# A gated mix of a long convolution and a two-layer network, with gradients: transfers cut by 128 partitions, ten shared staging rows, and no DMA turns in the last weight-gradient blocks

## The chip, the cores and the metric

The kernel runs on one core of a Trainium2 chip. The metric is the device time of one execution in microseconds; lower is better. A core has the engines PE (matrix multiply; its weight loads are listed as PEld), DVE, ACT, POOL and SP. Transfers are issued by SP, ACT and POOL, each on a queue of its own (in the profile q1 is SP's, q10 ACT's, q0 POOL's), and carried by 16 DMA engines that all queues share. An engine name with a q behind it (SPq) is that engine's own queue issuing a transfer.

## What is computed

The reference is the forward pass and all gradients of a mix of two branches. With u of 2048 positions x 448 channels, in bfloat16:

```python
g = sigmoid((u * gate_w).sum(-1))
A = A_re + 1j * A_im                      # 448 x 256, as B and C
P = exp((dt * A)[:, :, None] * l)         # l = 0 .. 2047, rounded to bfloat16
K = einsum("dn,dnl,dn->dl", C, P, dt * B).real
y = irfft(rfft(u, 4096) * rfft(K, 4096))[:2048] + u * Dskip
h = relu(x @ w1 + b1) ** 2                # 1792 wide
b = h @ w2 + b2
out = g * y + (1 - g) * b                 # x is u; out_0
```

out_1 is the gradient to u, out_2 to out_7 those to A, B and C, out_8 and out_9 to log_dt and Dskip, out_10 to out_13 those to w1, b1, w2 and b2, out_14 that to the gate. grad_out is the incoming gradient.

## The kernel before

D is 448, L 2048, F 1792, P 128, LT 16 (positions per partition), FT 14 (blocks of 128 of F), NG 4. All lines are those of the kernel before.

**Layout.** On chip, position 64 r + 16 g + t lies on partition 32 g + r, in slot t. In DRAM a partition's positions are one run; the partitions of one g are 64 positions apart, and the four g are 16 positions apart.

**The convolution as a two-step transform.** `fwd1` (L219 to L241) is the first step, along partitions: 8 groups, each of two pairs of matmuls with the constant F1, evacuated to a staging row of 128 x 4 x 448 by ACT and DVE, and stored to DRAM (gd) by two transfers of 64 partitions: one on `self.q2` (POOL, later ACT), one on SP. A staging row is reused when both of its stores have landed. `load_s1` reads gd back with the other index on partitions, `fwd2` is the second step. `inv1` and `inv1p` are the first inverse step; they store to hd. `load_hs` (L316 to L320) reads hd back, in which every load needs rows of all stores, and `inv2` is the last step.

**The stages, in order.**
- Start (L395 to L558). u, then grad_out (tile K), are loaded, 32 partitions at a time, alternately by SP and ACT. SP then issues six DMA turns (transposing transfers, L422) of A, B and C into tile X, then the constants M2, MI, Etw and sel. u goes through `fwd1` with four staging rows in tile F17, gd[0]; then DA = g * grad_out through `fwd1` with six rows in tile R32, gd[1]. The parameters' arithmetic on DVE (L529 to L551) makes dt * A and C * dt * B, `powers` (L617) their powers, stored as rec_d by ACT (L647). `transposed` (L471) turns u, and later DB = (1-g) * grad_out, on PE, with copies by ACT and DVE in turn, and spills them.
- First inverse (L690 to L736). The product of the spectra of u and DA, stored as hd[0] by L296. Its eight loads (L693, `both=True`, half on ACT, half on SP) fill four tiles (D and P); the matmuls at L713 sum them by rounded position; the sums go out to dk_d (L726) and come back as DK (L733). w1 is loaded behind them on SP (L697, L700), w2 by POOL (L1029).
- The main loop (L965 on) over 14 chunks of 32 channels builds K and the gradients of the parameters, on PE, DVE and ACT, between the two-layer network's matmuls (L584, L1021, L1084). The diff does not touch it.
- The output gradient again (tile Gt, L1276), K's spectrum through `fwd1` (gd[2]), M2 again, the loads of gd[2] (L1271) and of the spilled spectra (sp, L1207), all on SP's queue.
- Late products and inverses. `product(0, q)` makes hd[1], `product(1, q)` hd[2], each with `inv1`. Eight loads of hd (four per inverse, each both halves on SP) use a ring of three buffers that they share with the loads of sp. Each inverse step is followed by stores of output 0 (POOL, L1377) or output 1 (SP and ACT in turn, L1402), 32 partitions at a time.
- Weight gradients. `grad_w2` and `grad_w1` work on one block j of 128 of the 1792 rows: `gradrows` (L1146) loads the block (128 x 2048) by POOL, turns it on PE in 16 steps (L1163), copies by ACT (L1164) and multiplies in 16 matmuls (L1169). For `grad_w1` with j from 5 to 13 ("late"), POOL loads half of the block and SP loads the other half already turned, by a DMA turn (L1153) that is put behind the last load of hd.

**What sets the order.** The order of each engine's instructions is fixed when the program is built: a scheduler places them by its own estimates and the program's order; `tc.issue_after(x)` puts what is in it behind x. Each queue is worked in that order, and a waiting instruction holds what is behind it on its engine. A transfer of SP or ACT takes one of a few completion semaphores and waits while an earlier transfer still holds it.

Of the kernel before, what the change touches and what calls it, by code (L numbers as in the profile page):

```python
# [19 lines left out]
P = 128  # L20
# [7 lines left out]
NG = 4  # L28
# [135 lines left out]
class Ker:  # L164
    def __init__(self, tc, pool, psum):
        self.tc = tc
        self.nc = tc.nc
        self.pool = pool
        self.psum = psum
        self.evac_i = 0  # L170
        self.st_i = 0
        self.st_more = []
        self.q2 = tc.nc.gpsimd
        self.pair_i = 0
        self.pairs3 = True
        self.act_only = False
        self.stage_i = 0
        self.dma_i = 0
        self.n = 0
# [39 lines left out]
    def fwd1(self, rhs, gd, stage, act_first=0):  # L219
        nc = self.nc  # L220
        for hh in range(2):
            for q in range(4):
# [13 lines left out]
                for g2 in range(2):  # L236
                    dst = bass.AP(tensor=gd, offset=(j0base + 16 * g2) * 64 * D, ap=[[D, 64], [64 * D, 4], [1, D]])
                    d = (self.q2 if g2 == 0 else nc.sync).dma_start(dst, st[g2 * 64:(g2 + 1) * 64])
                    if g2 == 0:
                        last = d  # L240
        return last  # L241
# [74 lines left out]
    def load_hs(self, hd, q, hs, both=False):  # L316
        for hp in range(2):
            src = bass.AP(tensor=hd, offset=(8 * hp + 2 * q) * D, ap=[[64 * D, 64], [16 * D, 4], [1, 2 * D]])
            last = (self.nc.scalar if both and hp == 0 else self.nc.sync).dma_start(hs[64 * hp:64 * hp + 64].rearrange("p g x d -> p g (x d)"), src)
# [15 lines left out]
def kernel(ctx, tc, A_u, A_A_re, A_A_im, A_B_re, A_B_im, A_C_re, A_C_im, A_log_dt, A_Dskip,  # L335
# [34 lines left out]
    def tl(ap2d, g):  # L370
        return bass.AP(tensor=ap2d.tensor, offset=ap2d.offset + 16 * g * D, ap=[[64 * D, 32], [1, LT * D]])
# [26 lines left out]
    for h in range(2):  # L398
        for g in range(NG):
            src = bass.AP(tensor=u2.tensor, offset=u2.offset + (16 * g + 8 * h) * D, ap=[[64 * D, 32], [1, 8 * D]])  # L400
            (nc.sync if g % 2 == 0 else nc.scalar).dma_start(flat(U[32 * g:32 * g + 32, 8 * h:8 * h + 8]), src)
# [8 lines left out]
    for g in range(NG):  # L410
        (nc.sync if g % 2 == 0 else nc.scalar).dma_start(flat(G[32 * g:32 * g + 32]), tl(G2, g))
# [8 lines left out]
    for nm, src in (("Ar", A_A_re), ("Ai", A_A_im), ("Br", A_B_re), ("Bi", A_B_im), ("Cr", A_C_re), ("Ci", A_C_im)):  # L420
        r = carve(2 * D).rearrange("p (h d) -> p h d", h=2)
        nc.sync.dma_start_transpose(out=r, in_=src)  # L422
        raw[nm] = r
    load_const("M2", nc.sync)
    for nm in ("MI", "Etw", "sel"):
        load_const(nm, nc.sync)
    K.M2, K.MI, K.Et = ct["M2"], ct["MI"], ct["Etw"]
    sel = ct["sel"][:].rearrange("p (k m) -> p k m", k=4)
# [16 lines left out]
    stage = [[b[:, 1792 * i:1792 * i + 1792].rearrange("p (a d) -> p a d", d=D) for i in range(k)] for b, k in ((Fs, 4), (RA, 6))]  # L445
    K.fwd1(lambda j: U[:, j, 0:D], gd[0], stage[0], 5)
    u_ev, u_dv, u_f1 = K.last_ev, K.last_dv, K.last_f1
# [23 lines left out]
    def transposed(src, spill):  # L471
        nonlocal nti
        for t2 in range(LT // 2):
# [7 lines left out]
            cp = S.copy if t2 % 2 == 0 else V.tensor_copy  # L481
# [12 lines left out]
    lf1 = K.fwd1(lambda j: DA[:, j, :], gd[1], stage[1])  # L494
# [60 lines left out]
    with tc.issue_after(u_f1.ins):  # L555
        transposed(U, UT_d)
# [60 lines left out]
    def powers(gr):  # L617
# [29 lines left out]
        nc.scalar.dma_start(bass.AP(tensor=rec_d, offset=4 * gr * P * RS, ap=[[RS, P], [P * RS, nch], [1, RS]]), R)  # L647
# [22 lines left out]
    for q in range(4):  # L670
# [8 lines left out]
        if q == 0:  # L679
            with tc.issue_after(f10.ins):  # L680
                transposed(DB, DBT_d)
# [452 lines left out]
    rl = [SB[:, 1024 * i:1024 * i + 1024] for i in range(2)]  # L1134
    hl = [SB[:, 2048 * i:2048 * i + 2048].rearrange("p (t f) -> p t f", f=P) for i in range(1, 4)]
    JL = 5
# [9 lines left out]
    def gradrows(w, j, nb):  # L1146

        nonlocal hi, ni
        late = w == 1 and j >= JL
        if late:  # L1150
            raw_, hh = rl[hi % 2], hl[hi % 3]
            with tc.issue_after(lasths.ins):
                nc.sync.dma_start_transpose(out=hh[:, 8:16], in_=bass.AP(tensor=dhT_d, offset=j * P * L + 1024, ap=[[L, P], [1, 1024]]))  # L1153
        else:
            raw_, hh = hr[:, hi % 2], hn[:, hi % 2]
        hi += 1
        nl = L // 2 if late else L
        G_.dma_start(raw_, bass.AP(tensor=(rT_d if w == 0 else dhT_d), offset=j * P * L, ap=[[L, P], [1, nl]]))
        for th in range(1 if late else 2):
# [116 lines left out]
    for g in range(NG):  # L1276
        nc.sync.dma_start(flat(Gt[32 * g:32 * g + 32]), tl(G2, g))
# [26 lines left out]
    def load_hs(w, q):  # L1304
# [3 lines left out]
        K.last_hs = K.load_hs(hd[w], q, hs)  # L1308
# [7 lines left out]
    for j in range(FT):  # L1316
        grad_w2(j)
        if j == 8:
            for g in range(NG):
                with tc.issue_after(last_s1.ins):  # L1320
                    nc.sync.dma_start(U[32 * g:32 * g + 32, :, 0:D], tl(u2, g).rearrange("p (t d) -> p t d", d=D))
# [26 lines left out]
    for q in range(4):  # L1348
# [26 lines left out]
        for g in range(NG):  # L1375
            dst = bass.AP(tensor=o0.tensor, offset=o0.offset + (16 * g + 2 * q) * D, ap=[[64 * D, 32], [8 * D, 2], [1, 2 * D]])
            G_.dma_start(dst, ao[32 * g:32 * g + 32].rearrange("p (h x) d -> p h (x d)", h=2))  # L1377
# [5 lines left out]
    for q in range(4):  # L1383
        hs = hsn
        if q < 3:
            hsn = load_hs(2, q + 1)
            lasths = K.last_hs
# [12 lines left out]
        for g in range(NG):  # L1400
            dst = bass.AP(tensor=o1.tensor, offset=o1.offset + (16 * g + 2 * q) * D, ap=[[64 * D, 32], [8 * D, 2], [1, 2 * D]])
            K.dma().dma_start(dst, xo[32 * g:32 * g + 32].rearrange("p (h x) d -> p h (x d)", h=2))  # L1402
# [14 lines left out]
    for j in range(JS, JL):  # L1417
        grad_w1(j, NB)
    hi = 0
# [36 lines left out]
```

## Time and profile before

| what | value |
| --- | --- |
| median of three runs | 948.91 us (948.11 to 955.28) |
| profiled execution | 948.11 us |
| its span | 945.9 us |
| mean granted PE clock | 0.827 |
| DMA packets | 170814, 184.96 MB, mean 196 GB/s |
| of which on SP's queue | 121462 packets, 84.74 MB |
| hd loads on SP into the ring | 16 of 448 KB, median 6.4 us to landing |
| hd loads of the first inverse | 8 of 448 KB, 11.1 to 12.9 us to landing |

The span is the time from the first to the last instruction of the profiled execution; the rest of its time lies around it. In the profile, a row of an engine's timeline gives start and duration in us, engine and line, operation, the tiles written and read, the count, and in brackets the idle time before it with what ended it. The chain of waits goes back from the last instruction, at each step to what released it; its rows give start, length and what. A row on DMA packets gives their number, bytes and rate in a window, and a row that begins with a queue's name its packets, MB and share of the 16 engines' time.

### The profile page before, as it was taken

The numbers are of one execution on the slowest core, as the hardware profiler recorded it, in microseconds if no ns is written. First come the engines' busy times: TensorE is split into PE (matmuls) and PEld (weight loads), VectorE is DVE, ScalarE is ACT, GpSimd is POOL, SyncE is SP. The second block draws the span as 40 slices with busy tenths as digits, with TensorE's granted clock in tenths as the row PEclk, the third lists the DMA queues.
The fourth block names the chain that finished last, engine by engine and source line by source line (L and its number), as shares of the span: only waits on it lengthen the run. The fifth ranks groups of instructions, "written<-read, shape, count | busy, mean of one in ns | idle before, by whom it ended". The sixth has DMA issues, their size and how long they took to land.

```text
span 945.9 us, 18861 instructions
## 1 busy us (share of the span) xinstructions
PE 713.0 (75%) x7585; PEld 339.5 (36%) x7585; DVE 671.3 (71%) x1152; ACT 579.4 (61%) x927; POOL 191.8 (20%) x327
## 2 busy tenths in 40 slices
PE   3345675636878888888888897789868888949896
PEld 1112222214344443444444442444323334514343
DVE  4388885787489989999987899864329854258820
ACT  3436757725997859788687666564526654435553
POOL 2141000113202112021202311223211021433231
PEclk9776565768869889899967998899969788968899
DMA  8976476797536754547752974659998996689852
GB/s 187 265 241 242 159 303 256 277 319 229 121 80 125 150 133 116 106 104 167 153 120 75 239 173 119 128 140 277 331 379 260 267 300 188 189 224 243 216 148 73
DMA packets 170814, 184.96 MB, mean 196 GB/s; under 512 B 100467, under 2 KB 146968, under 8 KB 169800
## 3 DMA queue, kind: packets, MB, share of 16 engines
q1 hardware_dynamic: 121462, 84.74, 37.5%
q0 software_dynamic: 19904, 59.15, 19.3%
q10 hardware_dynamic: 29362, 39.88, 12.8%
q8 instruction: 59, 0.97, 0.4%
q14 instruction: 27, 0.22, 0.1%
HBM read 88.22 MB, written 73.13 MB: 171 GB/s over the span
## 4 chain that ended last, share of the span: by engine, by line
PE 31%; ACT 19%; DMA 17%; DVE 13%; issue 12%; POOL 3%; SPq 2%; ACTq 1%; POOLq 0%; DVEq 0%
PE psN L1021 6%; PE psF L1169 3%; DMA S<-rT_d 3%; ACT R L917 3%; PE psX L844 2%; PE psN L1084 2%; PE psN L584 2%; ACT S L591 2%; SPq L422 2%; PE psX L882 2%; PE psF L913 2%; ACT R L871 1%; DMA hd<-st 1%; DMA D<-hd 1%; DMA U<-in_A_u_dram 1%
## 5 line engine op out<-in xcount | busy, mean ns | idle before, releaser
L933 DVE TENSOR_TENSOR P<-R 128x2048 bf16<-128x2048 bf16 x42 | 49.5, 1219 | 24.4 <-ACT R L917 20.9
L917 ACT CAST R<-psF 128x1024 bf16<-128x1024 f32 x56 | 57.4, 1025 | 14.5 <-PE psF L913 14.3
L1169 PEld LDWEIGHTS <-S 128*128 128x128 bf16 x448 | 43.8, 104 | 59.8 <-issue 16.0
L1021 PE MATMUL psN<-D,S 128*128 128x448 bf16 x208 | 54.6, 397 | 6.4 <-ACT S L591 6.3
L1169 PE MATMUL psF<-U,S 128*128 128x448 bf16 x224 | 51.3, 379 | 2.1 <-ACT S L1164 2.0
L584 PE MATMUL psN<-S,U 128*128 128x512 bf16 x132 | 39.2, 412 | 8.5 <-ACT F L589 4.9
L913 PE MATMUL psF<-R,S 64*32 64x256 bf16 (+1 forms) x1344 | 38.3, 298 | 9.3 <-DMA R<-Y 4.5
L1084 PE MATMUL psN<-S,U 128*128 128x512 bf16 x126 | 39.1, 433 | 6.9 <-ACT D L1089 6.9
L773 DVE TENSOR_TENSOR X<-X,F 128x512 bf16<-128x512 bf16 (+1 forms) x70 | 37.4, 535 | 4.5 <-ACT F L807 2.6
L784 DVE TENSOR_TENSOR K<-K,F 128x2048 bf16<-128x2048 bf16 (+3 forms) x42 | 36.3, 865 | 4.9 <-ACT F L812 3.3
L207 DVE CAST K<-psN 128x448 bf16<-128x448 f32 x36 | 21.6, 620 | 25.0 <-PE psN L255 24.8
L1097 POOL DMA_DIRECT2D dhT_d<-D x28 | 20.2, 721 | 88.6 <-DVE D L1096 88.4
L785 DVE TENSOR_TENSOR F<-K,F 128x2048 bf16<-128x2048 bf16 (+3 forms) x42 | 35.9, 855 | 2.8 <-ACT F L814 2.8
L784 DVE TENSOR_TENSOR Y<-Y,F 128x2048 bf16<-128x2048 bf16 (+3 forms) x42 | 36.3, 865 | 1.6
L774 DVE TENSOR_TENSOR F<-X,F 128x512 bf16<-128x512 bf16 (+1 forms) x70 | 36.9, 527 | 0.6
L787 DVE TENSOR_TENSOR K<-K,F 128x2048 bf16<-128x2048 bf16 (+3 forms) x42 | 36.3, 865 | 1.3
L787 DVE TENSOR_TENSOR Y<-Y,F 128x2048 bf16<-128x2048 bf16 (+3 forms) x42 | 36.3, 864 | 1.3
L785 DVE TENSOR_TENSOR F<-Y,F 128x2048 bf16<-128x2048 bf16 (+3 forms) x42 | 35.9, 855 | 0.3 <-ACT F L814 0.3
L883 ACT COPY M<-psX 128x1024 bf16<-128x1024 bf16 x26 | 26.4, 1017 | 15.3 <-PE psX L882 15.2
L1021 PE MATMUL psN<-S,D 128*128 128x448 bf16 x168 | 35.7, 361 | 0.0
L1364 DVE SCALAR_TENSOR_TENSOR F<-psN,Y 128x448 bf16<-128x448 f32 x16 | 9.9, 619 | 35.7 <-PE psN L329 35.7
L1163 PEld LDWEIGHTS <-S 128*128 128x128 bf16 x376 | 25.5, 103 | 26.2 <-DMA S<-rT_d 9.4
(385 smaller groups left out, 1934.0 us busy)
## 6 DMA issues: line engine op xcount, KB each, us to landing
sp<-K ACTq DMA_DIRECT2D x8, 896.0 KB, 5.1
hd<-st ACTq DMA_DIRECT2D x16, 448.0 KB, 4.6
dhT_d<-D POOLq DMA_DIRECT2D x28, 256.0 KB, 5.1
R<-sp SPq DMA_DIRECT2D x8, 896.0 KB, 20.9
S<-rT_d POOLq DMA_DIRECT2D x14, 512.0 KB, 6.2
R<-hd SPq DMA_DIRECT2D x16, 448.0 KB, 6.4
rec_d<-F ACTq DMA_DIRECT2D x2, 1920.0 KB, 9.1
Y<-gd SPq DMA_DIRECT2D x4, 896.0 KB, 5.3
```

Source lines behind the costliest of these rows:

```text
L584: T_.matmul(ps[:], lhsT=w1w[:, dt, j * P:j * P + P], rhs=ub[:, dt], start=(dt == 0), stop=False, skip_group_check=True)
L773: V.tensor_tensor(out=hi4, in0=lo, in1=bcast_dims(pr, [0, (None, n), 1]), op=ALU.mult)
L774: V.tensor_tensor(out=Vv.rearrange("p (x a r) -> p x a r", x=2 * W2, r=2), in0=lo, in1=bcast_dims(pi, [0, (None, n), 1]), op=ALU.mult)
L784: V.tensor_tensor(out=hi, in0=lo, in1=bcast_dims(pr, [0, (None, n // 2), 1]), op=ALU.mult)
L785: V.tensor_tensor(out=Vv.rearrange("p (x a q) -> p x a q", x=rows, q=2), in0=lo, in1=bcast_dims(pi, [0, (None, n // 2), 1]), op=ALU.mult)
L787: return V.tensor_tensor(out=T4[:, :, :, n:2 * n], in0=T4[:, :, :, n:2 * n], in1=V4, op=ALU.add)
L913: T_.matmul(psz[32 * ii:32 * ii + m, t, 256 * s:256 * s + 256], lhsT=DKc[64 * t:64 * t + 64, s, g, 2 * ii:2 * ii + 1 + par].rearrange("p i ...
L917: S.copy(zb[:, :, :, gg].rearrange("p s t n -> p t s n"), psz[:].rearrange("p t (s n) -> p t s n", s=2))
L933: lastp = V.tensor_tensor(out=pr.rearrange("p s t g n -> p s t (g n)"), in0=zv, in1=(xb if r == 0 else rev_dim(xb, 2)), op=ALU.mult)
L1021: lastm = T_.matmul(ps[:, 0:D], lhsT=hblk[j][:, P * tt:P * tt + P], rhs=ws[:, j, :], start=(w == 1 and j == 0), stop=(j == FT - 1))
L1084: T_.matmul(ps[:], lhsT=w2Tw[:, jp, dt, j % 2], rhs=dblk[:, dt], start=(dt == 0), stop=False, skip_group_check=True)
L1169: lastm = T_.matmul(ps[:, 0:width], lhsT=hh[:, t, :], rhs=(DB2[:, t, :] if w == 0 else U[:, t, 0:D + 1]), start=(t == 0), stop=(t == LT - 1))
```

## The change

- `load_hs`: four transfers of 128 partitions (one per g), in place of two of 64.
- The loads of u: four transfers of 128 partitions (four slots each), in place of eight of 32. Those of grad_out, at the start and again as Gt: two each, in place of four. The stores of outputs 0 and 1: two of 128 partitions per step, in place of four of 32. In DRAM each of these starts with the four g. The second load of u (L1321) keeps its four transfers, position by position.
- The four and six staging rows become one ring of ten for both `fwd1`; the second half of DA's stores is issued by ACT instead of SP (`q3`).
- The parameters' turns and the constants are put behind the last store of u's spectrum on SP's queue.
- All eight copies of u's turn are ACT's; DB's stay in turn. The rec_d stores go from ACT to POOL.
- `gradrows` has no late form: all blocks are loaded whole by POOL and turned on PE; the blocks from 5 on use three PSUM banks in place of seven.

In the order as built, the first three loads of a late inverse (12 transfers) stand together on SP's queue behind the load of sp that the third product of the second inverse needs; after the last `inv2` PE has nine whole gradient blocks and part of a tenth.

```diff
     def load_hs(self, hd, q, hs, both=False):
-        for hp in range(2):
-            src = bass.AP(tensor=hd, offset=(8 * hp + 2 * q) * D, ap=[[64 * D, 64], [16 * D, 4], [1, 2 * D]])
-            last = (self.nc.scalar if both and hp == 0 else self.nc.sync).dma_start(hs[64 * hp:64 * hp + 64].rearrange("p g x d -> p g (x d)"), src)
+        for g in range(4):
+            src = bass.AP(tensor=hd, offset=(2 * q + 16 * g) * D, ap=[[8 * D, 2], [64 * D, 64], [1, 2 * D]])
+            last = (self.nc.scalar if both and g % 2 == 0 else self.nc.sync).dma_start(hs[:, g].rearrange("p x d -> p (x d)"), src)
...
-    def tl(ap2d, g):
-        return bass.AP(tensor=ap2d.tensor, offset=ap2d.offset + 16 * g * D, ap=[[64 * D, 32], [1, LT * D]])
+    def tl(ap2d, t0, n):
+        return bass.AP(tensor=ap2d.tensor, offset=ap2d.offset + t0 * D, ap=[[16 * D, NG], [64 * D, 32], [1, n * D]])
...
-    for h in range(2):
-        for g in range(NG):
-            src = bass.AP(tensor=u2.tensor, offset=u2.offset + (16 * g + 8 * h) * D, ap=[[64 * D, 32], [1, 8 * D]])
-            (nc.sync if g % 2 == 0 else nc.scalar).dma_start(flat(U[32 * g:32 * g + 32, 8 * h:8 * h + 8]), src)
+    for h in range(4):
+        (nc.sync if h % 2 == 0 else nc.scalar).dma_start(flat(U[:, 4 * h:4 * h + 4]), tl(u2, 4 * h, 4))
...
-    for g in range(NG):
-        (nc.sync if g % 2 == 0 else nc.scalar).dma_start(flat(G[32 * g:32 * g + 32]), tl(G2, g))
+    for h in range(2):
+        (nc.sync if h % 2 == 0 else nc.scalar).dma_start(flat(G[:, 8 * h:8 * h + 8]), tl(G2, 8 * h, 8))
...
-    stage = [[b[:, 1792 * i:1792 * i + 1792].rearrange("p (a d) -> p a d", d=D) for i in range(k)] for b, k in ((Fs, 4), (RA, 6))]
-    K.fwd1(lambda j: U[:, j, 0:D], gd[0], stage[0], 5)
+    stage = [b[:, 1792 * i:1792 * i + 1792].rearrange("p (a d) -> p a d", d=D) for b, k in ((Fs, 4), (RA, 6)) for i in range(k)]
+    K.fwd1(lambda j: U[:, j, 0:D], gd[0], stage, 5)
+    with tc.issue_after(u_st.ins):
+        for nm, src in (("Ar", A_A_re), ("Ai", A_A_im), ("Br", A_B_re), ("Bi", A_B_im), ("Cr", A_C_re), ("Ci", A_C_im)):
+            r = carve(2 * D).rearrange("p (h d) -> p h d", h=2)
+            nc.sync.dma_start_transpose(out=r, in_=src)
+            raw[nm] = r
+        load_const("M2", nc.sync)
...
-    lf1 = K.fwd1(lambda j: DA[:, j, :], gd[1], stage[1])
+    K.q3 = nc.scalar
+    lf1 = K.fwd1(lambda j: DA[:, j, :], gd[1], stage)
+    K.q3 = nc.sync
...
-        transposed(U, UT_d)
+        transposed(U, UT_d, (S.copy, S.copy))
...
-        nc.scalar.dma_start(bass.AP(tensor=rec_d, offset=4 * gr * P * RS, ap=[[RS, P], [P * RS, nch], [1, RS]]), R)
+        G_.dma_start(bass.AP(tensor=rec_d, offset=4 * gr * P * RS, ap=[[RS, P], [P * RS, nch], [1, RS]]), R)
...
-        late = w == 1 and j >= JL
-        if late:
-            raw_, hh = rl[hi % 2], hl[hi % 3]
-            with tc.issue_after(lasths.ins):
-                nc.sync.dma_start_transpose(out=hh[:, 8:16], in_=bass.AP(tensor=dhT_d, offset=j * P * L + 1024, ap=[[L, P], [1, 1024]]))
-        else:
-            raw_, hh = hr[:, hi % 2], hn[:, hi % 2]
+        raw_, hh = hr[:, hi % 2], hn[:, hi % 2]
...
-        for g in range(NG):
-            dst = bass.AP(tensor=o0.tensor, offset=o0.offset + (16 * g + 2 * q) * D, ap=[[64 * D, 32], [8 * D, 2], [1, 2 * D]])
-            G_.dma_start(dst, ao[32 * g:32 * g + 32].rearrange("p (h x) d -> p h (x d)", h=2))
+        for h in range(2):
+            dst = bass.AP(tensor=o0.tensor, offset=o0.offset + (8 * h + 2 * q) * D, ap=[[16 * D, NG], [64 * D, 32], [1, 2 * D]])
+            G_.dma_start(dst, ao[:, 2 * h:2 * h + 2].rearrange("p x d -> p (x d)"))
...
-    for j in range(JS, JL):
+    for j in range(JS, FT):
         grad_w1(j, NB)
-    hi = 0
-    for j in range(JL, FT):
-        grad_w1(j, NB + NT[0:4])
```

## The prediction, made before the changed kernel ran

> **What bounds the kernel now.** I read the page first, then the chain of waits stage by stage, then the engines' timelines where the diff acts, then the DMA answers for short windows. The sum is made against the profiled execution: 948.11 us, of which 945.9 us are the span. The median of the three runs is 948.91 us, so the two stand within 0.1%.
>
> ```profile
> PE 713.0 (75%) x7585; PEld 339.5 (36%) x7585; DVE 671.3 (71%) x1152; ACT 579.4 (61%) x927; POOL 191.8 (20%) x327
> DMA  8976476797536754547752974659998996689852
> PE 31%; ACT 19%; DMA 17%; DVE 13%; issue 12%; POOL 3%; SPq 2%; ACTq 1%; POOLq 0%; DVEq 0%
> ```
>
> No engine is full, and the chain changes hands: what counts is which wait ends last in the four stages that the diff touches. The start, from the chain of 0 to 75 us and from PE's timeline:
>
> ```profile
> 2.14 11.46 DMA U<-in_A_u_dram
> 19.58 5.89 SPq L422
> 33.56 3.94 DMA gd<-F
> 38.55 0.91 PE L229 MATMUL psF<-U,cb_F1BD 128*128 128x448 bf16 x2 [13.91 <-ACT F L216]
> 60.30 0.62 DVE L529 TENSOR_TENSOR R<-X,ldb 128x448 f32<-128x448 bf16 x1
> ```
>
> u lands at 13.6 us. Then SP issues the six parameter turns (L422) and the constants until 33.5 us, and the spectrum's stores wait behind them. With four staging rows, PE, ACT and DVE stand still from 24.6 to 38.5 us. The parameters' arithmetic starts on DVE at 60.3 us. The first inverse, from the chain of 180 to 262 us and PE's timeline:
>
> ```profile
> 190.40 4.97 DMA hd<-st
> 196.19 12.24 DMA D<-hd
> 214.38 11.28 DMA dk_d<-st
> 215.79 0.55 PE L713 MATMUL psN<-P,M 128*32 128x448 bf16 x3 [2.08 <-DMA P<-hd]
> ```
>
> Here nothing but transfers is on the chain: all hd[0] has to be stored, then all of it is read back (issued 195.5 us, the last tile 215.8 us), then dk goes out. The end, from PE's and SP's timelines:
>
> ```profile
> 758.74 0.37 SPq L1207 DMA_DIRECT2D R<-sp  x1
> 761.68 0.53 PE L327 MATMUL psN<-R,negI 128*128 128x448 bf16 x1 [0.63 <-ACT st L206]
> 797.56 3.20 PE L1169 MATMUL psF<-U,S 128*128 128x448 bf16 x16 [0.25 <-ACT S L1164]
> 802.32 3.20 PE L1169 MATMUL psF<-U,S 128*128 128x448 bf16 x16 [0.19 <-ACT S L1164]
> 892.40 0.56 PE L329 MATMUL psN<-R,cb_Etw 64*32 64x448 bf16 x8
> ```
>
> A full block of the weight gradients (16 turns, 16 matmuls) takes 4.76 us; the last inverse ends at 892.9 us and some nine blocks follow it, 53 us to the end of the span. Last, how a transfer is spread over the DMA engines, and what one engine moves. The window 940.45 to 941 us holds one transfer, the 14 rows of the bias gradient on SP's queue (q1); the window 207 to 211 us holds the loads of hd and no other data on two queues:
>
> ```profile
> q1 hardware_dynamic: 28, 0.00, 4.0%
> ```
>
> ```profile
> DMA packets 849, 1.44 MB, mean 361 GB/s; under 512 B 61, under 2 KB 831, under 8 KB 849
> ```
>
> The 28 packets are 14 of 256 bytes and 14 completion writes of 4 bytes: 14 engines took part, not 16. A second count: between 213 and 226 us SP's queue has 129 completion writes in the packet records. The three loads of w1 (128, 64 and 64 partitions) would write 16 each, four dk_d pieces whose destination has 16 rows outermost 16 each, one single row 1. That is 113; the other 16 belong to two pieces whose destination has 8 rows outermost and whose source has 32 partitions. So 8 engines each: the smaller outermost size decides. In the second window 16 engines moved 361 GB/s, 22.6 GB/s each.
>
> **The change part by part.**
>
> 1. *How the transfers are cut.* The new loads of u and of the output gradient, and the stores of outputs 0 and 1, have 128 partitions on chip but 4 rows outermost in DRAM; the new loads of hd have 2. By the counts above I take 4 and 2 engines: a continuation of 14, 8 and 1, which no row shows for 4 and 2. Whether successive transfers share the same engines is not settled either: from 225.48 us on, eight of SP's packets run one after another in two groups of four, each closed by a completion write, as two eight-row transfers on the same engine would, but two sixteen-row ones would look alike. One end is no effect at all (the loads as now), the other is all on the same 2 or 4 engines at 22.6 GB/s each. I take the second, since the counts are the nearest rows, and keep both.
>
> The row here is 129 completion writes. The Trainium skill, "DMA: Bandwidth & Descriptors", section "Why a DMA increments its semaphore by 16 and not by 1", says the same for any size (the largest count up to 16 that divides the outermost sizes of both sides), and adds that SP's and ACT's transfers go to the lowest-numbered engines, which no row here shows. Its section "Rules for kernel authors" advises one 128-partition transfer in place of two halves, which speaks for this change, and warns of an outermost size under 16, which speaks against it. By its advice on halves the loads of hd would take no longer and the sum would be the first rival's; by its rule on the outermost size, the forecast's.
>
> 2. *Start.* u is 1.835 MB: on 4 engines (90 GB/s) 20 us instead of 11.5, but a quarter lands at a time. It is all in at some 23 us, and the output gradient, as large, follows on the same engines at some 43 us, later still where u's spectrum stores (3.7 MB over 16 engines, 10 us each at 361 GB/s) mix in: 43 to 50 us. Gone is the 13.9 us stall: the turns are now behind the last store of u on SP, and ten rows are free. But DVE needs the gradient for DA, which it has at 41.8 us now; then 4 us of products and some 10 us of evacuations lead to 58 to 64 us for the parameters' arithmetic, against 60.3. The six turns (16.4 us of SP's queue now) and M2, issued from some 28 us on, are in by 50 to 58 us; SP's loads of the first spectra wait behind them. All eight copies of u's turn on ACT (1.02 us each, four of them moved from DVE at 0.68) fill ACT's wait for the gradient. The rec_d store (9 us to land) is issued by POOL instead of ACT, 1 us of POOL's queue, nothing behind it on ACT. Sum +3 us; bounds -14 (the stall gone, nothing new) and +12.
>
> 3. *First inverse.* 16 transfers of 229 KB, 3.67 MB, on 2 engines (45 GB/s): 81 us, with 4.4 us for the share of w2 (1.6 MB / 16 / 22.6 GB/s) that mixes in, and 2 to start: 88 us, where 20.3 us stand now. Nothing covers it: PE and ACT need the sums, and DVE runs out of work at 240.8 us already now. It gives back about 5 us, since w1 and w2 have mostly landed before dk goes out (11.28 us to land now, under w1 and w2). Sum +62; bounds 0 and +80 (packets at the 100 ns of the busiest part).
>
> 4. *The output gradient again (Gt).* On SP's queue its two loads stand between the last stores of gd[2] and the loads that the second transform needs. On 4 engines they hold those up by 8 to 18 us; PE has gaps of 6.4 and 3.0 us there (691 to 702 us) that take part of it. Sum +6; bounds 0 and +15.
>
> 5. *The late inverses.* Eight loads of 917 KB, 20.3 us each on 2 engines, on SP alone. The built order puts three of them together behind the sp load that is issued at 758.74 us now; hd[1] was ready at 748.2. So the first lands at 781 us (inverse now at 761.7: PE stands 19 us), then 801 and 821; the last sp load, behind the third, 824, its product and stores make hd[2] ready at some 850; then four loads to 932, and three quarters of output 1's stores (1.835 MB on 4 engines, 20 us) mix in: 947 us. In the built order nine and a half gradient blocks still stand behind the last inverse.
>
> 6. *The last nine blocks.* Each loses one DMA turn (1.5 to 3.9 us of SP's queue) and half a load, and gets 8 turns on PE (0.45 us) and one more copy on ACT (1.02 us, beside PE): 9 x 0.45 = 4 us. So 57 us behind the last inverse instead of 53. With item 5: 947 + 2 + 57 = 1006, +60; bounds +4 (loads as now) and +90 (loads shared with the blocks' own loads, 26 us each).
>
> Sum: 948.1 + 3 + 62 + 6 + 60 = **1079 us**.
>
> **The rivals.**
> - *No transfer is held up* (engines are not bound by the outermost size, or each transfer gets others). For it: all queues together reach 361 GB/s. Against it: the counts of 14 and 8. Then the stall at 24.6 us goes, -14 at most and -10 after what follows it, +4 for item 6: 942 us, the other side. It decides when the hd load of the first inverse lands within 26 us.
> - *The late loads are covered*: the scheduler's blocks keep PE busy and only the first wait of 19 us stays. For it: PE is 80% busy from 750 to 900 us. Against it: nine blocks are built behind the last load. 948 + 3 + 62 + 6 + 20 = 1039 us.
> - *The 2 engines also hold up the queues*: SP and ACT wait in order for a completion semaphore that a slow load still holds, so ACT's copies stop behind output 1's stores. Tail +100 in place of +60, first inverse +80: 1140 us.
>
> **How the numbers follow.** Forecast 0.50, late loads covered 0.18, queues held up too 0.17, no transfer held up 0.15. The first three all end slower; the low end takes item 3 at +50, start -10 and tail +25 (1013), the high end reaches the third rival: 1010 to 1145 us, which leaves out the fourth case, 0.15, and some of the third's upper part. About 1% is what a measurement of this kernel can tell from no change. The fourth case at 942 lies within 1% but for its best end, -14: faster 0.06, same 0.09, slower 0.85.
>
> **What would show it.** Right: the loads of u, Gt and hd reach some 90, 90 and 45 GB/s when alone, with 4, 4 and 2 completion writes each; PE's wait for the hd load at 190 us is near 80 us; SP's stores of gd are issued without the gap of 24 to 38 us; the last inverse comes 40 to 60 us later against the stage's start. Wrong: hd loads that still take 12 to 20 us would leave only the gain at the start; a tail that ends 53 us after the last gd work would move 40 us out of item 5.

## The result, and the profile after

| what | before | after |
| --- | --- | --- |
| median | 948.51 us (946.69 to 955.28, 4 runs) | 1148.72 us (1145.56 to 1152.38, 4 runs) |
| span of the profiled execution | 945.9 us | 1147.7 us |
| mean granted PE clock | 0.827 | 0.779 |
| ratio | | 1.2096, 95% interval 1.2026 to 1.2166 |

The medians take in every run; the ratios are worked out without runs more than 1.5% above the fastest of their kernel, and are not exactly the quotients of the medians.

The changed kernel is 21% slower. The forecast was 1079 us and its range ended at 1145. The direction and the number of engines were right; how much of the late loads' time would show was not.

The page of the changed kernel, the same lines as shown of before:

```profile
PE 747.0 (65%) x7657; PEld 348.6 (30%) x7657; DVE 668.5 (58%) x1148; ACT 591.8 (52%) x940; POOL 191.0 (17%) x323
DMA  4797568215364565556466576988852656323132
DMA 30%; PE 25%; ACT 16%; DVE 10%; issue 8%; ACTq 5%; SPq 5%; POOL 1%; DVEq 0%; POOLq 0%
```

DVE is as busy in us as before, ACT 12 us and PE 34 us busier, yet the span has grown by 202 us: waiting was added. On the chain DMA went from 17% to 30%, and the two queues (SPq, ACTq), 3% before, hold 10%. In the row of DMA shares the eighth and ninth of 40 slices show 2 and 1 and the last six 1 to 3: few of the 16 engines are busy there, and in the eighth and ninth the chain is nothing but transfers and their issuing.

Where the time came in, by the start of the same instruction in both traces (us; the last column is what the stretch before it added):

| mark | before | after | added |
| --- | --- | --- | --- |
| parameters' arithmetic on DVE begins | 60.3 | 61.8 | +1.5 |
| last sum of the first inverse on PE | 218.7 | 292.8 | +72.6 |
| K's spectrum: first `fwd1` matmul | 654.4 | 724.8 | -3.7 |
| second transform: first weight load of `fwd2` (PEld) | 690.4 | 784.6 | +23.8 |
| last late inverse's last matmul | 892.6 | 1079.9 | +93.1 |
| last gradient matmul | 937.3 | 1137.9 | +13.3 |

The first matmul of `fwd2` starts with that weight load before, and 2.2 us after it in the changed kernel.

The start, from the chain of 0 to 75 us (start, length, what):

```profile
2.77 42.88 DMA K<-in_grad_out_dram
...
49.58 0.33 SPq L239
...
49.95 2.33 SPq L443
...
61.79 7.69 DMA X<-in_A_C_im_dram
```

u's first half lands at 17.3 us and the output gradient (K) at 45.7; the turns (L443), now behind u's stores, are issued from 50 us on. The stall of 24 to 38 us is gone, and the slow loads have taken its place.

The first inverse, from the chain of 185 to 310 us; the loads of hd are line 322 now:

```profile
194.14 2.20 DMA hd<-st
...
200.81 9.96 ACTq L322
210.80 9.17 ACTq L322
...
224.25 15.27 ACTq L322
239.55 9.16 ACTq L322
248.75 39.66 DMA P<-hd
```

Issuing a load took some 0.6 us before; here single issues take 4 to 15 us, as if the queue took no more before earlier packets were gone, and ACT itself stands in L322 until 258 us. The last tile lands at 288.4 us: 89 us from the first issue, where 20.3 us stood. What the transfers move, from the DMA answer for 225 to 235 us, in which nothing but hd loads of the two queues is on the way:

```profile
DMA packets 278, 0.49 MB, mean 49 GB/s; under 512 B 4, under 2 KB 278, under 8 KB 278
q1 hardware_dynamic: 138, 0.24, 6.7%
q10 hardware_dynamic: 140, 0.25, 6.4%
```

Two queues together move 49 GB/s and take 13.1% of the time of 16 engines, which is that of 2.1 engines: some 24.5 GB/s each (22.6 in the trace of before). SP's and ACT's transfers therefore use the same two engines. The packet records show the same count in another way: the three transfers that ACT's queue carries between 4 and 45 us (two quarters of u, half of the gradient) end in 12 completion writes, 4 each.

The late part, from the chain of 735 to 1147 us:

```profile
739.33 27.41 DMA gd<-P
768.14 0.71 SPq L248
768.89 31.46 DMA R<-sp
...
870.07 19.58 DMA R<-hd
...
898.72 24.18 DMA R<-sp
...
964.72 3.29 DMA hd<-st
...
975.97 21.44 DMA R<-hd
...
1000.22 18.90 DMA R<-hd
...
1028.40 14.37 DMA R<-br_d
...
1057.32 16.13 DMA R<-hd
```

The first row is Gt's place: the last store of gd, on SP's queue behind Gt's first load, takes 27 us to land (of its 16 completion writes twelve come by 744.3 us, four between 759.2 and 766.7). Only then are the loads of gd issued, and the first sp load behind them takes 31 us. Then come the hd loads at some 20 us each. hd[2] is complete only at 968 us, and its four loads fill the time to 1073.5. In the kernel before, its last store is issued at 841.6 us, by ACT's timeline:

```profile
841.62 0.37 ACTq L314 DMA_DIRECT2D hd<-st  x1
```

The row at 870.07 is not a wait for that load's data. Behind it in the chain stands a store of hd[2] that ACT issues at 889.73. From ACT's timeline, then from PE's:

```profile
856.35 0.53 ACT L207 CAST st<-psN 128x448 bf16<-128x448 f32 x1 [10.66 <-DMA R<-hd]
889.73 0.37 ACTq L317 DMA_DIRECT2D hd<-st  x1
890.14 1.02 ACT L1158 ACTIVATE S<-psS 128x1024 bf16<-128x1024 bf16 x1 [23.67 <-DMA R<-hd]
```

```profile
891.22 3.17 PE L1163 MATMUL psF<-U,S 128*128 128x448 bf16 x8 [14.11 <-ACT S L1158]
```

Twice, for 10.7 and 23.7 us, ACT stands at a store of hd[2]. In the trace each of the two stores takes the completion semaphore of an hd load that SP had issued (at 840.34 and 870.07) and goes out when that load has landed (855.8 and 889.7). ACT's copies stop behind it, and PE behind them: between 840 and 968 us two of PE's waits, of 7.2 and 14.1 us, end with these copies, and only one, of 3.6 us, with an hd load itself.

The stretch of the late inverses by windows, first before and then after (us, then the busy time of PE, PEld, DVE, ACT and POOL, the PE clock, DMA share and GB/s):

```profile
757.00:893.00 136.00, 109.51 (x721) 51.20 (x719) 76.22 (x176) 68.05 (x130) 41.87 (x74) 0.84 0.81 230
```

```profile
839.70:1080.00 240.30, 130.86 (x743) 54.87 (x742) 67.44 (x145) 70.77 (x131) 35.67 (x60) 0.69 0.42 134
```

PE's busy time differs by 21 us, its idle time by 83 (26.5 before, 109.4 after). And the end, from the same chain:

```profile
1124.28 3.21 PE psS L1163 x16
1127.57 0.54 ACT S L1175
1128.11 0.92 ACT S L1158
...
1129.68 3.21 PE psF L1163 x16
```

The last blocks follow each other every 5.4 us.

### The profile page after: what moved, and what is told of

It reads as the page before. It is cut to its first block, busy times and chain, and to the rows that moved or that the text cites. A ratio compares the mean times of both kernels' runs of the same rounds, so it can differ in the third digit from the quotient of the medians.

```text
span 1147.7 us, 19007 instructions
## 1 busy us (share of the span) xinstructions
PE 747.0 (65%) x7657; PEld 348.6 (30%) x7657; DVE 668.5 (58%) x1148; ACT 591.8 (52%) x940; POOL 191.0 (17%) x323
## 4 chain that ended last, share of the span: by engine, by line
DMA 30%; PE 25%; ACT 16%; DVE 10%; issue 8%; ACTq 5%; SPq 5%; POOL 1%; DVEq 0%; POOLq 0%
DMA R<-hd 7%; DMA R<-sp 5%; PE psN L1025 5%; ACTq L322 4%; DMA K<-in_grad_out_dram 4%; DMA P<-hd 3%; SPq L322 3%; DMA gd<-P 2%; PE psN L588 2%; PE psX L848 2%; ACT R L921 2%; PE psF L1163 2%; PE psF L917 1%; PE psX L1163 1%; DMA R<-br_d 1%
## 5 line engine op out<-in xcount | busy, mean ns | idle before, releaser
L1163 PEld LDWEIGHTS <-S 128*128 128x128 bf16 x448 | 45.5, 107 | 89.1 <-issue 37.0
L921 ACT CAST R<-psF 128x1024 bf16<-128x1024 f32 x56 | 57.3, 1023 | 13.3 <-PE psF L917 13.3
L1025 PE MATMUL psN<-D,S 128*128 128x448 bf16 x208 | 49.5, 372 | 6.3 <-ACT S L595 6.3
L818 ACT ACTIVATE F<-recy 128x640 bf16<-128x640 bf16 (+2 forms) x30 | 19.7, 700 | 61.0 <-DMA P<-hd 61.0
L332 PE MATMUL psN<-R,cb_Etw 64*32 64x448 bf16 x128 | 20.1, 466 | 42.5 <-DMA R<-hd 42.5
L1158 ACT ACTIVATE S<-psS 128x1024 bf16<-128x1024 bf16 x24 | 24.8, 1031 | 35.4 <-DMA R<-hd 23.7
L313 PE MATMUL psN<-P,cb_MI 64*128 64x448 bf16 x128 | 28.0, 412 | 21.0 <-ACT st L207 7.4
L270 DVE TENSOR_TENSOR F<-R,K 128x1792 bf16<-128x1792 bf16 x8 | 8.7, 1089 | 54.3 <-DMA R<-br_d 48.5
L258 PEld LDWEIGHTS <-M 128*64 128x64 bf16 x192 | 14.1, 131 | 80.8 <-issue 53.3
L1240 DVE TENSOR_TENSOR X<-U,X 128x256 f32<-128x256 bf16 (+1 forms) x24 | 9.2, 420 | 50.1 <-ACT X L1247 49.8
L788 DVE TENSOR_TENSOR Y<-Y,F 128x2048 bf16<-128x2048 bf16 (+3 forms) x42 | 36.3, 865 | 1.6
```

The lines of the kernel that those rows point to most:

```text
L788: V.tensor_tensor(out=hi, in0=lo, in1=bcast_dims(pr, [0, (None, n // 2), 1]), op=ALU.mult)
L921: S.copy(zb[:, :, :, gg].rearrange("p s t n -> p t s n"), psz[:].rearrange("p t (s n) -> p t s n", s=2))
L1025: lastm = T_.matmul(ps[:, 0:D], lhsT=hblk[j][:, P * tt:P * tt + P], rhs=ws[:, j, :], start=(w == 1 and j == 0), stop=(j == FT - 1))
L1163: lastm = T_.matmul(ps[:, 0:width], lhsT=hh[:, t, :], rhs=(DB2[:, t, :] if w == 0 else U[:, t, 0:D + 1]), start=(t == 0), stop=(t == LT - 1))
```

## The experiments

Theory: the smaller outermost size of a transfer's two sides sets how many engines carry it, and the loads of hd (2), then those of u, the gradient and Gt and the output stores (4), are the loss. Rivals: transfers of 128 partitions in these pieces are slow as such (A); the cause is not hd but the other edits (B). In all runs the kernel before ran on the same chip; one point of ratio is 9.4 us, and most ratios are known to within 0.7 points.

**Rows outermost, the same bytes.** The values are of other rows.

```diff
-            src = bass.AP(tensor=hd, offset=(2 * q + 16 * g) * D, ap=[[8 * D, 2], [64 * D, 64], [1, 2 * D]])
+            src = bass.AP(tensor=hd, offset=(2 * q + 16 * g) * D, ap=[[64 * D, 64], [8 * D, 2], [1, 2 * D]])
```

> The changed kernel; only the source of the hd loads is written with the 64 rows outermost and the two halves inside (64 x 2 instead of 2 x 64). Same four loads of 128 partitions, same bytes, same packets of 1792 bytes; the rows arrive in another order, so the inverses work on other rows. Theory (the smaller outermost size sets the engines): 16 engines again, each group of hd loads lands in 10 to 25 us, the first inverse's wait falls by some 57 us and the late part by 60 to 110 us: 985 to 1030 us. Rival A (loads of 128 partitions in four pieces are slow as such): within 1% of 1149 us. Rival B (hd is not the cause, but the other cuts and the lost DMA turns): within 2% of 1149 us.

Measured: 972.05 us, ratio 1.0314 (1.0217 to 1.0411). Rival A falls, and B too: same partitions, number, size and packets, and 18 points are gone. That is more than the theory's 985 to 1030 us allowed. The DMA answer for 205 to 215 us of this kernel, in the middle of the first inverse's loads:

```profile
DMA packets 2313, 3.84 MB, mean 384 GB/s; under 512 B 265, under 2 KB 2237, under 8 KB 2312
```

384 GB/s where the changed kernel has 49.

**Four rows outermost.**

```diff
-            src = bass.AP(tensor=hd, offset=(2 * q + 16 * g) * D, ap=[[8 * D, 2], [64 * D, 64], [1, 2 * D]])
+            src = bass.AP(tensor=hd, offset=(2 * q + 32 * (g % 2) + 2048 * (g // 2)) * D, ap=[[8 * D, 4], [64 * D, 32], [1, 2 * D]])
```

> The changed kernel; the hd loads read all the same rows, cut so that 4 rows are outermost instead of 2 (other rows to each partition, so the inverses work on other rows). Theory: 4 engines, twice the rate (90 to 100 GB/s): the 81 us of the first inverse's loads become some 40, late loads 10 us in place of 20 each: 1050 us, between 1020 and 1085. Rival A and rival B: within 2% of 1149 us.

Measured: 1050.2 us, ratio 1.1155 (1.1071 to 1.1240), as the theory had it.

**The old loads of hd in the changed kernel, and the new ones in the kernel before.** The edit is the first hunk of the diff, undone, and done alone.

> The changed kernel with the hd loads of the kernel before (two of 64 partitions, 64 rows outermost). Theory: as with rows outermost, 985 to 1030 us, the same within 1% as that kernel. Rival A: much below the kernel with rows outermost, which stays at 1149. Rival B: within 2% of 1149 us.

> The kernel before with the new hd loads alone (2 rows outermost). Theory: the first inverse some 60 to 70 us later and the late part 60 to 110 us longer: 1065 to 1125 us. Rival B: within 2% of 949 us. If parts add, this run's excess over 949 and the drop of the kernel with two halves from 1149 are equal.

Measured: 969.4 us, ratio 1.0318 (1.0253 to 1.0382), the same as with rows outermost and again below the 985 us expected; and 1105.96 us, ratio 1.1790 (1.1706 to 1.1875). Undoing takes off 17.8 points, doing it alone adds 17.9: the part adds up. Of the loss of 21 points hd is 18.

**The first inverse alone undone.**

```diff
+        if both:
+            return self.load_hs_old(hd, q, hs, both)
```

> The changed kernel, with only the first inverse's eight hd loads (SP and ACT) cut as before; the late ones keep 2 rows outermost. Theory (first inverse +62 in the prediction, some 70 by the marks of the profile after): 1080 us, between 1070 and 1095, so that the late loads still cost about 100 us. Rival (the late loads are mostly covered and the first inverse is the bulk): 1010 to 1040 us.

Measured: 1083.05 us, ratio 1.1496 (1.1430 to 1.1561). So the first inverse's loads cost 6.0 points (57 us) and the late ones 11.8 (111 us): the bulk is in the late part.

**The three other parts, each alone in the kernel before.** The edits are the hunks of the change: ring, order of the turns and copies; the cuts with four g outermost; the form of the last blocks.

> The kernel before with the start's changes alone: the ring of ten staging rows, the parameter turns and constants behind the last store of u's spectrum, DA's second stores by ACT, all copies of u's turn on ACT, the rec_d stores by POOL; all transfers cut as before, the last blocks in their late form. Theory (the stall of 13.9 us goes, nothing new): 8 to 12 us faster, ratio 0.988 to 0.992. Rival (the parameters' turns, now behind the stores, end last): ratio 1.00 to 1.01.

> The kernel before with the cuts of u, of the two loads of the output gradient and of the stores of outputs 0 and 1 alone (4 rows outermost); hd loads, start and last blocks as before. Theory: u and the gradient land some 9 and 15 us later (+10 to +15), Gt holds up the second transform by 15 to 25 us, the stores of output 1 mix with the last hd loads (0 to +8): 25 to 45 us longer, ratio 1.026 to 1.047. Rival (they are hidden, the excess of 30 us left with the old hd loads is the last blocks' form): ratio under 1.01.

> The kernel before with the last nine blocks in the full form alone (whole block by POOL, turned on PE, three PSUM banks). Theory: 9 blocks times 0.45 us of PE turns and the lower number of banks: +4 to +10 us, ratio 1.004 to 1.01. Rival (the blocks' form is what is left of the excess): +25 to +35 us, ratio 1.026 to 1.037.

Measured: 929.76 us, ratio 0.9848 (0.9791 to 0.9905), a kernel that beats both; 992.14 us, 1.0494 (1.0418 to 1.0570); 953.73 us, 1.0111 (1.0073 to 1.0149). The start gains 1.5 points where 0.8 to 1.2 were expected, the cuts cost 4.9 where 2.6 to 4.7 were, and the last blocks 1.1 where 0.4 to 1.0 were; all three intervals reach into the expected range. For the start, DVE's timeline of that run has the first of the parameters' products at 44.2 us instead of 60.3:

```profile
44.20 0.62 DVE L535 TENSOR_TENSOR R<-X,ldb 128x448 f32<-128x448 bf16 x1 [3.02 <-DMA X<-in_A_B_re_dram]
```

With the new cuts of the second of these runs alone the same product starts at 81.4 us. Alone these are -16.1 and +21.1 us; in the changed kernel the two together make +1.5. The four parts add to 22.4 points, the whole has 21.0.

**Gt.** First its cut alone undone, then its two loads issued by POOL (`G_`) with the new cut.

> The changed kernel with the second load of the output gradient (Gt) cut as before, four loads of 32 partitions. Theory (4 engines need 18 us for the two loads, and the loads of gd[2] and of the first spilled spectra on SP's queue end behind them): 20 to 30 us faster than the changed kernel, 1119 to 1129 us. Rival (the prediction's own term, 6 us, the rest of the step at the second transform being something else): 1140 to 1146 us.

> The changed kernel with Gt's two loads issued by POOL instead of SP, still 4 rows outermost. Theory (what costs is the order within SP's queue: a short load behind a slow one ends after it): 15 to 30 us faster, 1119 to 1134 us. Rival (what costs is that 4 of the 16 engines are busy, on whatever queue): 0 to 8 us faster, 1141 to 1149 us.

Measured: 1132.76 us, ratio 1.1998 (1.1949 to 1.2046), and 1146.8 us, ratio 1.2116 (1.2038 to 1.2193). Undone, the second transform starts 23 us earlier in the trace, as the theory had it, but only 1.0 point (9 us, to within 8) is left at the end, between what the two expected. By POOL the stretch before it is 13 us shorter in the trace, and nothing is gained at the end: in the chain of this run POOL issues Gt (Y), and its own stores and loads behind that are what the rest waits for:

```profile
745.28 0.73 POOL Y L1271
...
754.76 15.10 DMA dhT_d<-D
...
770.41 18.74 DMA S<-rT_d
```

**The loads of sp by POOL.** Is the hd load's place on SP's queue what counts?

```diff
-        nc.sync.dma_start(t_, bass.AP(tensor=sp_d[w], offset=q * 8 * D, ap=[[16 * 2 * D, P], [1, 8 * D]]))
+        (G_ if w else nc.sync).dma_start(t_, bass.AP(tensor=sp_d[w], offset=q * 8 * D, ap=[[16 * 2 * D, P], [1, 8 * D]]))
```

> The changed kernel with the four loads of the second product's spilled spectra issued by POOL instead of SP, so that the third no longer stands behind twelve slow hd loads on the same queue. Theory (order within the queue): that load takes under 12 us in place of 24, hd[2] is ready earlier, 10 to 25 us faster, 1124 to 1139 us. Rival (the hd loads themselves are all that counts): within 5 us of 1149.

Measured: 1149.7 us, ratio 1.2194 (1.2128 to 1.2261): no gain, as the rival had it. The loads now land in 6.8 to 8.7 us, where the third took 24. hd[2]'s last store is issued 10 us earlier than in the changed kernel (964.72), by ACT's timeline; the last late inverse ends 4 us earlier, and at the end nothing is left:

```profile
954.90 0.37 ACTq L317 DMA_DIRECT2D hd<-st  x1
```

The chain of this run has another short load in the place of the one removed:

```profile
938.47 4.38 DMA U<-in_A_B_re_dram
942.84 20.71 DMA U<-s_d
```

**Eight rows outermost.** As with four, with `offset=(2 * q + 1024 * g) * D, ap=[[8 * D, 8], [64 * D, 16], [1, 2 * D]]`.

> The changed kernel; the hd loads read the same rows with 8 rows outermost (other rows to each partition, so the inverses work on other rows). Theory: 8 engines, half the time again: first inverse's loads 20 us in place of 81, like the kernel before, late loads 5 us each, hidden behind the gradient blocks: 970 to 1000 us. Rival (the time falls by half with each doubling all the way, nothing is hidden): 1010 us, half way from 1050 to 972.

Measured: 1002.96 us, ratio 1.0591 (1.0528 to 1.0655). It lies between the two expectations (the theory's upper end 1000, the rival's 1010) and 2.8 points above 16 engines, so little is hidden. The number of engines can be counted in these traces: each hd load of the first inverse raises its completion semaphore once just after the issue and then 2, 4 or 8 times with 2, 4 or 8 rows outermost; with 64 it is 16 times. The series of ratios with 16, 8, 4 and 2 engines is 1.031, 1.059, 1.116 and 1.210: steps of 2.8, 5.6 and 9.4 points, 26, 53 and 89 us, each known to about 1.1 points. The hd loads are 11.0 MB in all. At 24.6 GB/s per engine (two move 48 to 50) they take 28, 56, 112 and 224 us, so the steps of transfer time are 28, 56 and 112 us: from nine tenths down to four fifths of it shows up in the kernel's time.

**What sets the late part?** Two theories, each with a kernel: X, all the bytes on the low engines; Y, short loads behind slow ones on SP's queue. For X the stores of outputs 0 and 1 are swapped like this; for Y the loads named in the expectation are issued by `G_`.

```diff
-            dst = bass.AP(tensor=o1.tensor, offset=o1.offset + (8 * h + 2 * q) * D, ap=[[16 * D, NG], [64 * D, 32], [1, 2 * D]])
+            dst = bass.AP(tensor=o1.tensor, offset=o1.offset + (8 * h + 2 * q) * D, ap=[[64 * D, 32], [16 * D, NG], [1, 2 * D]])
```

> The changed kernel; only the stores of outputs 0 and 1 are written with the 32 rows outermost and the four g inside (the outputs' rows land in another order). No engine waits for these stores before the end. Theory X (the late part lasts as long as everything that the lowest engines have to carry): 3.67 MB fall from a quarter to a sixteenth on each of these engines, 0.69 MB at some 24 GB/s = 28 us less, 15 to 28 us faster, 1120 to 1134 us. Theory Y (the late part is a chain of short loads and engines that wait in order behind the slow hd loads): 0 to 8 us faster, 1141 to 1149 us.

> The changed kernel; the late loads of the second product's spectra, of the branch's rows (br_d, from the second group on) and of the parameter sums (s_d, t_d) are issued by POOL, so that on SP's queue nothing but output stores mixes with the hd loads, still 2 rows outermost. Theory Y (order within SP's queue): 40 to 60 us faster, 1090 to 1110 us. Theory X (the load of the two engines): 0 to 10 us faster, 1139 to 1149 us.

Measured: 1145.09 us, ratio 1.2134 (1.2085 to 1.2182), and 1152.87 us, ratio 1.2183 (1.2138 to 1.2229). Neither gains. X and Y both fall as the one cause. In the second of these kernels SP issues nothing but hd loads from 843 to 1040 us, and its timeline merges them into one row:

```profile
843.32 196.88 SPq L322 DMA_DIRECT2D R<-hd  x29
```

But they do not follow each other without a break: within this row SP issues nothing from 907 to 933 and from 946 to 971 us. The second gap ends when hd[2]'s last store has landed, which is issued only 3 us earlier than in the changed kernel, by the chain of this run:

```profile
961.70 8.97 DMA hd<-st
970.86 0.49 SPq L322
```

So a free queue does not help the last four loads: they wait for what PE and ACT have to do first. ACT's wait at a store of hd[2] is there in both kernels (22.6 and 23.1 us, 23.7 in the changed one).

**All cuts with rows outermost.** The same swap at u, the gradient, Gt, hd and the output stores.

> The changed kernel; the loads of u, of both loads of the output gradient, of hd, and the stores of outputs 0 and 1 all keep their 128 partitions, number and size, but have 32 (hd: 64) rows outermost instead of 4 (hd: 2); rows come to other partitions, so its values are of other rows. PE and DVE work in the same order. Theory: the whole loss is in the outermost size; what is left is the start's gain (ratio 0.985 alone) and the last blocks' cost (1.011 alone): 0.99 to 1.00 of the kernel before. Rival (transfers of 128 partitions lose something as such): 1.01 to 1.03.

Measured: 923.66 us, ratio 0.9799 (0.9770 to 0.9828), faster than both kernels and below what the theory expected (the start's and the last blocks' ratios multiply to 0.996). The whole loss is in the order of the DRAM side's dimensions; with 16 engines the 128-partition form even seems to gain 1.6 points, and the parameters' products start at 39.8 us. Its layout of rows is not one that the rest of the kernel can use as it stands.

**PE's own order.** In the order built some twelve gradient blocks stand between the first late inverse and the last step that makes hd[2]. They were moved behind that step (`K.last_i1` is the last matmul of `inv1`), with the parameter gradients that follow them:

```diff
-    for j in range(FT):
-        grad_w2(j)
+    for j in range(4):
+        grad_w2(j)
...
+    for j in range(4, FT):
+        with tc.issue_after(K.last_i1.ins):
+            grad_w2(j)
```

> The changed kernel with twelve gradient blocks moved: the blocks of the second weights from j = 4 on, the first two of the first weights and the parameter gradients behind them are placed after the last inverse step that makes hd[2], instead of in between. In the order built, eleven of them stand between the last inverse's steps and twelve blocks behind it (nine and a half in the changed kernel). Theory Z (PE works in order: while it waits for the first slow hd loads it can not run the blocks that stand in front of hd[2]'s last step, so hd[2] is stored late and its four loads, some 105 us, start late): hd[2]'s last store comes 40 to 50 us earlier after the first late inverse step (100 us now), the blocks lie under the four loads, the tail is some 13 us longer: 1105 to 1130 us. Rival (the bytes on the two engines set the stage's length whatever PE does): 1140 to 1155 us.

> The same move of the twelve blocks, in the kernel in which all cuts have rows outermost (16 engines). Control: with short hd loads there is nothing to gain, the tail is longer by some blocks: between 5 us faster and 20 us slower than that kernel, 0.975 to 1.00 of the kernel before.

Measured: 1153.86 us, ratio 1.2232 (1.2181 to 1.2283); the control 930.94 us, 0.9860 (0.9816 to 0.9904). hd[2]'s last store, first in the changed kernel and then with the blocks moved (ACT's timelines):

```profile
964.72 0.37 ACTq L317 DMA_DIRECT2D hd<-st  x1
```

```profile
926.23 0.37 ACTq L317 DMA_DIRECT2D hd<-st  x1
```

The step is right: hd[2] is stored 38 us earlier, so the blocks in front of it on PE had held it up. Its four loads and the last inverses then take 13 us longer, and the last late inverse ends 25 us earlier. But the time does not fall to what theory Z had; it is what the rival had, though not for the rival's reason, as the stretch up to the last inverse is 25 us shorter. All of that is given back behind it: the last gradient matmul comes 26 us later after the last inverse (17 us later in the control, where this was the expected cost of the move). The chain there is made of the moved parameter gradients and blocks. What was a wait in the middle became work at the end.

## Why the prediction was off

- **Engines by outermost size: right.** 4 and 2 engines, the same ones for successive transfers and for both queues, at some 24.5 GB/s each instead of the 22.6 assumed (the window from which that came also holds 18 packets of w1, of 3584 bytes, beside the loads of hd). The rule was a continuation of 14, 8 and 1; the runs with 2, 4, 8 and 16 settle it, and they agree with the Trainium skill, "DMA: Bandwidth & Descriptors", section "Why a DMA increments its semaphore by 16 and not by 1". The advice of its section "Rules for kernel authors", one 128-partition transfer in place of two halves, holds only together with the warning of the same section: 1.210 against 1.031 for the same 128 partitions.
- **Start, +3: right in size (+1.5), with some luck.** It is a sum of two larger terms. The stall's end was put at -14 at most; it brought -16.1 at the parameters' products and 1.5 points (14 us) alone. The new cuts alone moved the products by +21.1, and the two do not simply add.
- **First inverse, +62: right.** Its loads took 89 us where 88 were worked out. The marks show 69 up to the end of the main loop; undone in the changed kernel it is 57 us, and in the kernel before the new hd loads make the second transform 62.5 us later.
- **The output gradient again, +6, bounds 0 and +15: too small.** The second transform came 24 us later. The loads' own 18 us were counted, but PE's gaps (9.4 us) were taken to swallow part of them, and the sum went by 6. Gt's loads were put behind the last stores of gd[2]; in the order built the first stands in front of three of them, so the last store took 27 us to land, and the loads of gd and of sp came behind it. At the end 9 us remain.
- **Late inverses and last blocks, +60, bounds +4 and +90: this is the step that failed, with +106.** The first three loads went as worked out, to within some 7 us. The error is in what follows: "its product and stores make hd[2] ready at some 850". In the kernel before, the last store of hd[2] is issued at 841.6 us, so three loads of 20 us each were let move it by less than 10 us, as if nothing else waited while they ran. Measured from the second transform's start (94 us later than before) hd[2] was ready at 968 - 94 = 874 us: the last sp load landed 5 us later than worked out, and from there hd[2] took 45 us, where 26 were allowed. Two things stand in its way. Some twelve gradient blocks are in front of its last steps on PE; with these moved it was stored 38 us earlier. And ACT, which makes the copies for these blocks, stood 34 us at its own stores of hd[2] until hd loads had landed, with PE behind it; that is in the trace, but no run took it away. Then the four loads took 105 us (97 with their mixing), 6 us more passed until the last inverse was through, and the tail was 9 us longer than the 59 predicted. That is 24 + 8 + 6 + 9 = 47 us, the 46 by which the term was missed.
- **In one number.** From 16 engines to 2 the late loads (7.34 MB) take 131 us longer. The prediction let 54 us of that move the last inverse. In the runs in which the late loads alone differ (the first inverse alone undone, and all hd loads as before) the last inverse moves by 99 us from the second transform's start, and the kernel's time by 111 us (85% of 131). The blocks that could cover the loads were ordered in front of what the next loads depend on.
- **The last blocks.** 4 us were predicted for nine blocks, 1.1 points (10 us) measured alone. The second copy on ACT is not beside PE: the fence above shows copy, turn's copy and matmuls following each other, 5.4 us a block, where the kernel before has 8.4 us for two.
- **The rivals.** "No transfer held up" (942) and "late loads covered" (1039) fall. "Queues held up too" (1140; its terms add to 1137) came nearest in time, and the waits that it named are there: ACT was held for 58 us while it issued the first inverse's loads, and later for 34 us by completion semaphores that slow loads held, its copies behind it. But this was at stores of hd[2]; output 1's stores on ACT were issued in 0.6 us each. The runs that gave the short loads another queue left this wait as it was (and with the blocks moved ACT still stands 10.5 and 18.9 us at stores of hd[2]), so they do not speak against this rival, and what it costs at the end was not tried.

**What stays open.** Why neither fewer bytes on the low engines nor short loads on another queue nor another order shortens the whole: where one wait fell, another wait or work behind it took its place. That it is one knot of loads, ACT's held stores, PE's order and the work behind it is argued from the chains, not shown by a run; a kernel whose stores of hd share no semaphore with the loads would be the next to try. Where the 1.6 points of the kernel with all rows outermost come from was not tried either.

## What to carry to other kernels

Before a transfer is made "wider" on chip, read the DRAM side's first dimension: 2 or 4 there meant 2 or 4 engines here, with 128 partitions on chip, and the order of two dimensions was worth 23 points. When a load becomes long, do not take a busy engine as its cover; follow the engine's order, ask which of its work may run before the load has landed, and which other transfer waits for the semaphore that the load holds. Undo a bundled change part by part: one of its parts alone was 1.5% faster than the kernel before.

## What the runs showed of the hardware

- When SP and ACT were given transfers on two engines, only the first two or so were issued quickly: after them an issue took 4 to 15 us in the first inverse instead of some 0.6, and on ACT that time was lost to its other work. Only how long it took is shown, not how many packets the queue holds.
- Transfers that use all engines were slowed by those in front of them on the queue: the third sp load took 24 us behind hd loads on SP and 6.8 to 8.7 us by POOL, and a store of gd behind a load on four engines had twelve of its 16 completion writes within 5 us and the other four after 20 to 27.
- The granted PE clock was lower where PE was idle more: 0.84 in the stretch of the late inverses before, 0.69 after, and a matmul of `inv2` (64 x 448) took 0.53 us after long waits, where 0.36 us are usual.
